# Writing out every engine's order with a small planner in an attention-plus-GLU block

## Chip, cores, metric

One core of one Trainium2 chip. The metric is device time in microseconds (us) of one execution; lower is better. Ratios are the mean time of one kernel's fast runs over that of the other's fast runs of the same rounds, so they are not quite the ratio of the medians quoted beside them. Medians are of all runs, those of state slow included (4 of the changed kernel's 20, and some of the kernel before); ratios and profiles are of fast runs alone, unless the text says otherwise.

## The reference

`x` is 2048 rows of 640 bf16 values. It is normalized once and goes through two branches, which are added to it:

```python
xn = layernorm(x)
q, k, v = split(xn @ wqkv)                # 32 heads of 20
# each position looks at itself and 7 others, 2 rows apart (dilated window of 8)
logits[s, w] = q[s] . k[s - 2*w] * 20**-0.5   # -1e9 where s - 2*w < 0
attn = softmax(logits over w)
A = (sum over w of attn[s, w] * v[s - 2*w]) @ wo
B = ((xn @ w_gate) * (xn @ w_up)) @ w_down    # hidden size 1536
return x + A + B
```

## The kernel before

It works in four chunks of 512 rows (four tiles of 128). Matmuls are on TensorE (PE). The window's products and weighted sums are on VectorE (DVE), PSUM copies on ScalarE (ACT), loads and stores mostly from SyncE's queue (SP). The order on each engine is found by the framework's scheduler from the order of the program. The parts that matter, with cuts:

```python
# the V weights are permuted first thing, ScalarE and GpSimd by turns
for i in range(KT):
    eng = nc.gpsimd.tensor_copy if i % 2 == 0 else nc.scalar.copy
    eng(out=wvp[:, i, :]..., in_=wst[:, i, :]...)

def vproj(c, xnT):
    for ttl in range(CH):
        v_t = cpool.tile([P, D], BF, name="v_t")          # pool default: 2 buffers
        for n0 in (0, N2):
            ...                                           # 5 matmuls into PSUM
            nc.scalar.copy(v_t[:, n0 : n0 + N2], ps[:, 0:N2])
        nc.sync.dma_start(out=vD[...], in_=v_t[:])        # V rows to DRAM

def weights(c):                                           # ... for g in range(2):
    for j in range(JL):                                   # 4 products, 4 buffers
        pt = apool.tile([P, KT, CS], BF, name="pw", tag="pw", bufs=4)
        nc.vector.tensor_tensor(pt[:], qT[:], kT[:, :, off : off + CS], ALU.mult)
    ...                                                   # 20 matmuls sum them by head
    nc.scalar.activation(e[:, g, :], lps[:], ACT.Exp, scale=scale)

def attend(c, ttl):
    v8 = apool.tile([P, W, D], BF, name="v8")             # 8 reloads of V, shifted rows
    for w in range(W):
        nc.sync.dma_start(out=v8[:, w, :], in_=vD[r0 : r0 + P, :])
    ...                                                   # weights, product, three adds

for c in range(NCH):                                      # after chunks 0 and 1 are projected
    for ttl in range(CH):
        attend(c, ttl)
    glu(c)
    if c + 2 < NCH:
        load_x(c + 2); proj(c + 2)
    if c + 1 < NCH:
        weights(c + 1)
    for ttl in range(CH):
        finish(c, ttl)                                    # down and output projection, residual
```

The softmax here doesn't subtract the row's maximum and nothing guards it: scores larger than these inputs give would overflow.

## Time and profile before

| | before |
|---|---|
| median of the first 6 runs | 310.88 us (308.91 to 313.74) |
| span in the profile | 306.5 us |
| first Q matmul to last matmul | 17.5 to 301.2 us |
| dense TensorE work, from pitches (start of one matmul to start of the next) | 265.6 us |

TensorE's dense work (the prediction builds that number) is 87% of the span, so the question is what fills the rest. The lines that show it are in the prediction. In rows of 40 digits each digit is the busy share of one slice of the span in tenths (9 is 90% or more); PEclk is TensorE's granted clock in tenths of full speed. Its columns are line, engine, operation, out<-in, shapes, count; busy time and mean ns; idle time of the engine ahead of it and what ended that:

```profile
L202 ACT CAST v_t<-psv 128x320 bf16<-128x320 f32 x32 | 13.2, 426 | 9.2 <-DMA vD<-v_t 5.5 <-PE psv L197 3.3
```

ScalarE stood 5.5 us, in eight waits, for a store of V to free one of two buffers. In the kernel before nothing behind it was urgent, and no wait of TensorE names it.

### The profile page before, as it was taken

How to read it: one execution, taken by the hardware profiler on the slowest of the kernel's cores; microseconds unless marked ns; L12 is line 12 of the kernel's file. 1: busy time of each engine (PE TensorE's matmuls, PEld its weight loads, DVE VectorE, ACT ScalarE, POOL GpSimd, SP SyncE). 2: the span in 40 equal slices, each digit the busy share in tenths (PEclk: the TensorE clock that was granted, in tenths of full speed). 3: DMA queues.
4: the chain of work that ended last, by engine and by line, in shares of the span. 5: the costliest groups of instructions: out<-in, count | busy, mean ns of one | idle time of the engine just before them, and what ended most of it. 6: DMA issues, size and time to landing. Idle time of an engine off the chain costs nothing.

```text
span 306.5 us, 4647 instructions
## 1 busy us (share of the span) xinstructions
PE 276.0 (90%) x1786; PEld 156.7 (51%) x1786; DVE 196.1 (64%) x277; ACT 123.4 (40%) x221; POOL 45.5 (15%) x92
## 2 busy tenths in 40 slices
PE   0279859999999999999996999999999999999993
PEld 0268524554444467754443467754445674444672
DVE  5223868799988126289999009169999418999311
ACT  1276515655567550035555550025553003555000
POOL 7543000261303001210000001220000121000120
PEclk9999969999999999999999999999999999999999
DMA  7999496825550021225554010225556123540111
GB/s 220 373 370 340 146 288 209 244 90 171 167 150 28 0 88 43 85 84 170 159 172 148 2 64 21 88 86 173 171 171 173 43 87 99 171 118 2 44 51 37
DMA packets 31479, 40.97 MB, mean 134 GB/s; under 512 B 3282, under 2 KB 30432, under 8 KB 31456
## 3 DMA queue, kind: packets, MB, share of 16 engines
q1 hardware_dynamic: 29888, 35.40, 37.3%
q0 software_dynamic: 1568, 5.26, 5.4%
q8 instruction: 14, 0.23, 0.3%
q14 instruction: 9, 0.07, 0.1%
HBM read 35.39 MB, written 5.26 MB: 133 GB/s over the span
## 4 chain that ended last, share of the span: by engine, by line
PE 48%; DVE 31%; DMA 8%; SPq 4%; issue 3%; ACT 3%; POOLq 0%; POOL 0%; DVEq 0%
PE psqk L179 15%; DVE prod L265 13%; DVE pw L223 5%; DVE prod L271 4%; PE psv L197 4%; SPq L243 4%; DMA wst<-in_A_wqkv_dram 3%; DVE hT L303 3%; PE lps L227 3%; DVE prod L272 2%; ACT xnT L160 2%; PE psu L294 2%; PE psg L288 1%; PE pso L277 1%; PE pst L159 1%
## 5 line engine op out<-in xcount | busy, mean ns | idle before, releaser
L223 DVE TENSOR_TENSOR pw<-qT,kT 128x2560 bf16<-128x2560 bf16 x32 | 46.0, 1481 | 25.8 <-ACT v_t L202 14.8
L288 PE MATMUL psg<-xnT,wg 128*128 128x512 bf16 x240 | 60.5, 379 | 0.0
L294 PE MATMUL psu<-xnT,wu 128*128 128x512 bf16 x240 | 60.3, 379 | 0.0
L299 ACT CAST gs<-psg 128x512 bf16<-128x512 f32 x48 | 28.1, 586 | 69.7 <-PE psg L288 36.5
L179 PE MATMUL psqk<-xnT,wqk 128*128 128x512 bf16 (+1 forms) x250 | 45.1, 343 | 0.8 <-ACT xnT L160 0.8
L316 PEld LDWEIGHTS <-hT 128*128 128x128 bf16 x384 | 37.0, 98 | 16.9 <-issue 2.2
L301 ACT CAST us<-psu 128x512 bf16<-128x512 f32 x48 | 28.1, 585 | 23.8 <-PE psu L294 23.5
L294 PEld LDWEIGHTS <-wu 128*128 128x128 bf16 x240 | 23.3, 98 | 26.8
L328 POOL DMA_DIRECT2D out_dram<-osb x16 | 8.8, 550 | 189.5 <-DVE osb L325 178.9
L288 PEld LDWEIGHTS <-wg 128*128 128x128 bf16 x240 | 23.2, 98 | 26.1
L179 PEld LDWEIGHTS <-wqk 128*128 128x128 bf16 x250 | 25.1, 101 | 20.5 <-issue 1.9
L271 DVE TENSOR_TENSOR prod<-prod 128x2560 bf16<-128x2560 bf16 x16 | 23.7, 1484 | 0.0
L197 PE MATMUL psv<-wvp,xnT 128*128 128x320 bf16 x160 | 22.4, 299 | 0.0
L159 PE MATMUL pst<-selb,xn_t 128*128 128x128 bf16 x80 | 8.2, 253 | 15.7 <-POOL rstd L151 9.0
L146 DVE BATCH_NORM_STATS2 stats<-x_t 128x6 f32<-128x320 bf16 x32 | 14.1, 468 | 11.4 <-DMA x_t<-in_A_x_dram 11.3
L303 DVE TENSOR_TENSOR hT<-gs,us 128x512 bf16<-128x512 bf16 x48 | 19.9, 415 | 0.1
L197 PEld LDWEIGHTS <-xnT 128*128 128x128 bf16 x160 | 15.7, 98 | 6.5
L321 PEld LDWEIGHTS <-oT 128*128 128x128 bf16 x160 | 15.6, 98 | 6.6 <-issue 0.6
L227 PE MATMUL lps<-pw,Ek 128*32 128x512 bf16 x160 | 14.9, 409 | 4.3 <-DVE pw L223 4.3
L187 ACT CAST qT<-psqk 128x512 bf16<-128x512 f32 (+1 forms) x25 | 12.5, 500 | 11.9 <-PE psqk L179 11.9
L202 ACT CAST v_t<-psv 128x320 bf16<-128x320 f32 x32 | 13.2, 426 | 9.2 <-DMA vD<-v_t 5.5
L187 ACT CAST kT<-psqk 128x512 bf16<-128x512 f32 (+1 forms) x25 | 12.5, 500 | 9.1 <-PE psqk L179 9.1
(213 smaller groups left out, 291.8 us busy)
## 6 DMA issues: line engine op xcount, KB each, us to landing
x_t<-in_A_x_dram SPq DMA_DIRECT2D x16, 160.0 KB, 4.2
xr<-in_A_x_dram POOLq DMA_DIRECT2D x16, 160.0 KB, 2.6
vD<-v_t SPq DMA_DIRECT2D x16, 160.0 KB, 1.8
out_dram<-osb POOLq DMA_DIRECT2D x16, 160.0 KB, 2.1
wg<-in_B_w_gate_dram SPq DMA_DIRECT2D x2, 960.0 KB, 11.6
wu<-in_B_w_up_dram SPq DMA_DIRECT2D x2, 960.0 KB, 13.4
wd<-in_B_w_down_dram SPq DMA_DIRECT2D x1, 1920.0 KB, 15.6
wqk<-in_A_wqkv_dram SPq DMA_DIRECT2D x2, 800.0 KB, 7.1
```

The costliest lines, as they stand in the source:

```text
L179: nc.tensor.matmul(ps[:, 0:n], lhsT=wqk[:, i, r * D + j * P : r * D + (j + 1) * P], rhs=xnT[:, i, t0 : t0 + n], start=(i == 0), stop=(i == ...
L187: nc.scalar.copy(dst[:, j, o : o + n], ps[:, 0:n])
L197: nc.tensor.matmul(ps[:, 0:N2], lhsT=xnT[:, i, tcols(ttl)], rhs=wvp[:, i, n0 : n0 + N2], start=(i == 0), stop=(i == KT - 1),)
L223: nc.vector.tensor_tensor(pt[:], qT[:], kT[:, :, off : off + CS], ALU.mult)
L265: nc.vector.tensor_tensor(prod[:].rearrange("p w (j h) -> p w j h", j=Dh, h=H), v8[:].rearrange("p w (j h) -> p w j h", j=Dh, h=H), a16[:, ...
L271: nc.vector.tensor_tensor(prod[:, 0:4, :], prod[:, 0:4, :], prod[:, 4:8, :], ALU.add)
L288: nc.tensor.matmul(pg[:], lhsT=wg[:, i, f * P : (f + 1) * P], rhs=xnT[:, i, :], start=(i == 0), stop=(i == KT - 1),)
L294: nc.tensor.matmul(pu[:], lhsT=wu[:, i, f * P : (f + 1) * P], rhs=xnT[:, i, :], start=(i == 0), stop=(i == KT - 1),)
L299: nc.scalar.copy(gs[:], pg[:])
L301: nc.scalar.copy(us[:], pu[:])
L303: nc.vector.tensor_tensor(h[:], gs[:], us[:], ALU.mult)
L316: nc.tensor.matmul(ps[:, 0:N2], lhsT=hT[f][:, tcols(ttl)], rhs=wd[:, f, n0 : n0 + N2], start=(f == 0), stop=False,)
```

## The change

The intent: TensorE should never stand for the attention chain of VectorE. The automatic order is switched off for all five engines. A small planner in the kernel simulates TensorE and VectorE with assumed durations while the program is built, and emits each operation at the moment when its simulated engine is free. TensorE has a main list of blocks (Q/K, V, gate/up, final projection); head sums, spreads and transposes ("burst") go between blocks when the plan says their input is ready. VectorE has one chain; gate products and residuals ("quick") slip in. PSUM is shared out anew, gate copies have 2 buffers (were 3), `e` has 2 (was 1), `oT` 6 (were 5). GpSimd forms 1/std for two or four tiles at once. The core of the diff, with cuts:

```diff
-    ps_log = ctx.enter_context(tc.tile_pool(name="ps_log", bufs=2, ...))
+    ps_log = ctx.enter_context(tc.tile_pool(name="ps_log", bufs=1, ...))
+    ps_e = ctx.enter_context(tc.tile_pool(name="ps_e", bufs=1, ...))
+    ctx.enter_context(tc.manual_schedule(engines={PE, DVE, Activation, SP, Pool}))
...
+    zt = cpool.tile([P, D], BF, name="zt", tag="v_t")   # zeros ahead of V; had a buffer of its own
...
+    def load_w1():
+        load_x(1)
+        ...                       # wg, wu in halves, then wo_perm, then wd
...
+    def run():
+        t = {"pe": 8.0, "dve": 3.0}
+        while main or chain or burst or quick:
+            ...
+            eng = "pe" if t["pe"] <= t["dve"] else "dve"
+            extra, base = (burst, main) if eng == "pe" else (quick, chain)
+            extra.sort(key=lambda o: o[3]())
+            pick = None
+            if extra and extra[0][3]() <= t[eng]:
+                pick = extra.pop(0)
+            elif base and base[0][3]() <= t[eng]:
+                pick = base.popleft()
+            ...
+            name, emit, took, _, after = pick
+            emit()
+            t[eng] += took
+            done[name] = t[eng] + 0.2
...
+                def product(g=g, j=j):
+                    pt = apool.tile([P, KT, CS], BF, name="pw", tag="pw", bufs=4)
...
+                def after(t, g=g, j=j, heads=heads, headed=headed):
+                    if j == JL - 1:
+                        burst.append((("heads", c, g), heads, 1.2, lambda t=t: t + 0.4, headed))
+                dve(("pw", c, g, j), product, 1.45, when(("qk", c)), after)
...
+    norm(0, 2)
+    side(load_w1)
+    norm(1, 4)
+    side(lambda: [permute_v(i, nc.gpsimd.tensor_copy if i % 2 == 0 else nc.scalar.copy)
+                  for i in range(KT)])
     weights(0)
+    side(lambda: (want_v8(0), want_v8(1), load_x(2)))
+    norm(2, 4)
+    attend(0)
+    weights(1)
+    side(lambda: load_x(3))
+    norm(3, 4)
+    attend(1)
+    weights(2)
+    weights(3)
+    attend(2)
+    attend(3)
+
+    qk(0, 2); vproj(0); qk(1, 1); vproj(1); glu(0); finish(0)     # one call a line
+    qk(2, 1); vproj(2); qk(3, 1); vproj(3); glu(1); finish(1)     # in the kernel
+    glu(2); finish(2); glu(3); finish(3)
+    run()
```

## The prediction

> **What bounds the kernel now.** I read the page's head and slices first, then the chain that ended last for the pitch of each kind of matmul, then stretches where a slice showed TensorE short of full, and last the timeline of VectorE in an attention stretch.
>
> ```profile
> PE 276.0 (90%) x1786; PEld 156.7 (51%) x1786; DVE 196.1 (64%) x277; ACT 123.4 (40%) x221; POOL 45.5 (15%) x92
> PE   0279859999999999999996999999999999999993
> DVE  5223868799988126289999009169999418999311
> PEclk9999969999999999999999999999999999999999
> ```
>
> A slice is 306.5/40 = 7.7 us. PE is full except in the first two slices, the stretch of slices 4 to 5 and one digit 6 at about 161 us. DVE swings between 9 and 0: it has 110 us of idle time in all, but stretches in which it is the full engine. So TensorE bounds the kernel, with holes where it waits for VectorE, ScalarE and the start.
>
> The 276.0 is an overlapping count, so I build the dense time from pitches in the chain (start, length, what, how many matmuls):
>
> ```profile
> 3.69 10.11 DMA wst<-in_A_wqkv_dram
> 13.82 2.54 ACT wvp L133 x2
> 17.70 12.03 PE psqk L179 x100
> 47.05 10.99 PE psqk L179 x50
> 83.15 1.08 PE psg L288 x5
> 106.48 5.43 PE psv L197 x40
> 111.91 1.19 PE lps L227 x20
> 117.83 1.63 PE pso_1357 L316 x12
> 119.46 0.68 PE pso_1357 L321 x5
> ```
>
> Sum: Q and K 12.03 + 3 x 10.99 = 45.0; V 4 x 5.43 = 21.7; gate and up 4 x 24 x 1.08 = 103.7; output projection 32 x (1.63 + 0.68) = 73.9; head sums 8 x 1.19 = 9.5; 32 groups of five transposes at about 0.3 (start-to-start 56 to 66 ns) = 9.6; 32 small matmuls that spread the weights at 0.07 = 2.2. Together 265.6 us. Dense work runs from 17.0 to 301.4 us = 284.4, so holes after the start cost about 19 us; 17.0 go by before it and 5.1 (residual, store, landing) after it.
>
> Two of those lines say where the start goes: ScalarE permuted the V weights (waiting 10 us for their load) ahead of the copies that the first Q matmul needed. The larger holes (stretch, then busy of PE, PEld, DVE, ACT, POOL, clock, DMA):
>
> ```profile
> 35.00:47.00 12.00, 7.72 (x64) 3.57 (x63) 7.61 (x10) 4.41 (x8) 0.00 (x0) 0.72 0.85 252
> 160.00:167.00 7.00, 4.42 (x51) 2.49 (x51) 6.92 (x10) 4.38 (x7) 0.00 (x0) 1.00 0.64 188
> 38.53 0.38 PE L227 MATMUL lps<-pw,Ek 128*32 128x512 bf16 x1 [0.83 <-DVE pw L223]
> 42.73 2.29 PE L227 MATMUL lps<-pw,Ek 128*32 128x512 bf16 x17 [0.82 <-DVE pw L223]
> ```
>
> In the first, PE takes its head sums one product at a time as DVE makes them (1.4 us each), and the granted clock fell to 0.72. Its useful work there is 2.4 head sums + 1.3 transposes + 0.2 spread, about 4 us of 12: 8 lost. In the second about 4 are lost: transposes wait for the last attention output. Some 3 to 4 more go near 231 to 240 us (head sums again), 2 near 93, and about 0.4 for most attention outputs.
>
> **What the Trainium skill says.** "TensorE: Matmul & The Clock Gate", Part 1, gives start-to-start of N/2.4 GHz + 2.5 ns warm, half the clock cold, warm after about 3.4 us of activity. The trace agrees: 216 ns at N=512, 136 at 320, 109 at 256, and 213 at N=256 in the first 2.3 us of Q. A dense block can't be improved by order; a cold start costs a little over 1 us wherever it falls. The same page (architectural detail) has the queues of ScalarE, VectorE and GpSimd as strict FIFO; the trace agrees in that 10 us ScalarE wait with ready copies behind it. So the written order is binding: one operation too early stops everything behind it. "Perfetto Trace Analysis", Optimization Strategy, advises interleaving regimes with different busiest engines; that is the change's aim.
>
> **The change part by part.** Arithmetic, shapes and instruction counts stay, but for GpSimd's rstd on two or four tiles at once.
>
> *Start.* x lands from 3.07 us (first statistics). Two tiles' statistics end at 5.3, rstd about 6.4, scaling 7.4, transposes and two 0.69 copies about 8.9. The first half of the Q/K weights was issued at 2.64 and landed 6.2 later: 8.8. Permuting V no longer stands ahead. Q can start at about 9.0 in place of 17.5: 8.5 gained. Against it: V weights land at 13.8 but are permuted only behind the statistics of chunk 1, whose x lands after them, about 14; 4.3 of statistics, 1.0 of rstd, then GpSimd's three copies of 1.30 end near 23, while PE could start V at about 21. Loss 2 to 3.
>
> *Attention threaded.* The order on PE is Q/K and V of chunks 0 and 1, gate/up 0, projection 0, Q/K/V 2 and 3, then gate/up and projection 1, 2, 3; head sums, transposes and spreads are put between blocks about when VectorE should have delivered. VectorE gets one chain, with gate products and residuals slipped in.
>
> ```profile
> 261.98 0.36 DVE L254 RECIPROCAL rs<-eT 128x32 f32<-128x32 f32 x1 [0.35 <-PE eT L249]
> 262.37 0.42 DVE L256 TENSOR_TENSOR a_2868<-eT,rs 128x256 bf16<-128x256 f32 x1
> 262.83 2.83 DVE L265 TENSOR_TENSOR prod<-v_2854,a_2868 128x5120 bf16<-128x5120 bf16 x1
> 265.91 1.48 DVE L271 TENSOR_TENSOR prod<-prod 128x2560 bf16<-128x2560 bf16 x1
> 267.65 0.82 DVE L272 TENSOR_TENSOR prod<-prod 128x1280 bf16<-128x1280 bf16 x1
> 268.50 0.49 DVE L274 TENSOR_TENSOR o_2874<-prod 128x640 bf16<-128x640 bf16 x1
> ```
>
> By start-to-start, one tile without gate products takes 0.39 + 0.46 + 2.75 + 1.40 + 0.74 + 0.41 = 6.15 us; the planner assumes 0.75 + 2.8 + 1.45 + 0.8 + 0.45 = 6.25. Products are 1.40 against 1.45, gate products 0.33 against 0.4; its PE blocks 1.08, 0.68 and 17 x 0.136 = 2.31 equal the chain's. So the plan should hold. Laying its chain along the PE order by hand: products of chunk 0 from about 24 us, attention 0 about 42 to 73 while projection 0 is due at 77; attention 1 ends near 125, needed at 160; attention 2 near 180, just ahead of projection 2; attention 3 has 30 us of slack. VectorE never has to be the bound.
>
> *New or remaining waits on PE.* (a) V permutation: 2.5. (b) Four product buffers: the fifth product of a chunk waits for the first head sum (0.4 lag + half a block 0.5 + 1.2 + 0.2 = 2.3 us), which the planner doesn't count; the second head sum stands in PE's order 0.9 after the planned product, so PE waits 1.4 less what VectorE gained on the plan (2 to 3%), about 0.8 x 4 = 3. (c) Four normalization transposes share two PSUM buffers with 0.69 us copies: 0.7 x 3 = 2. (d) Projection's last gate products, held behind a 2.8 us operation: 0.7 x 3 = 2. (e) Placing the other 40 or so insertions, at 0.05: 2. Sum 11.5, in place of 19.
>
> *Sum.* 9.0 + 265.6 (its Q of chunk 0 holds the cold start; less 0.7 for two transpose groups before it) + 11.5 + 5.1 = 290.5 us of span, 16 below. The six timed runs' median lies 4.4 above the profiled span and the profiled run itself 1.75; with 2.5 to 3: 293.
>
> **The rivals.** (1) *VectorE becomes the bound.* Its 196.1 us busy are far below 290, and the plan's constants are slightly long. But PE is in order, so every lag is a PE stall; if the chain lags 2 us at each of its 24 stages (chunks' products, tiles), some 15 us return: 305. The 0 digits of DVE in the old slices speak against it: there is slack to fill. (2) *PE runs nearly dense*: the waits (b) to (e) fall within the slack, and 4 us remain: 283 of span, 286. For it, the constants look calibrated on this chip; against it, the buffers are as few as before, and fewer for head sums (PSUM 2 to 1) and gate copies (3 to 2). (3) *The start is bandwidth-bound*: DMA share is 1.06 and 364 GB/s between 17 and 30 us. If x of chunk 1 or the V copies come late, (a) grows to 6: 297.
>
> **Range and chances.** The eight gained at the start are the safest part; the holes at 35 to 47 and 160 to 167 are nearly as safe, since other PE work is ordered there. Giving back all of it needs rival 1 in full. I take 293, with 286 (rival 2) and 302 (most of rival 1) as ends. Faster by over 2% (below 304.7): 0.94; within 2%: 0.05; slower: 0.01.
>
> **What would show it.** Right: first Q matmul near 9 us; V of chunk 0 starts 2 us or so after Q and K end; no PE digit under 9 from slice 4 on; the clock stays at full after its warm-up; DVE's zeros fill until about 215 us and then thin out; PE's leftover waits name pw, the xnT copies and gate products, a few us together; last matmul near 285. Wrong: waits of 1 us or more at most attention transposes, a second clock drop, or gate-copy waits on ScalarE that pass to PE through full PSUM buffers.

## The result, and the profile after

The changed kernel took 310.46 us (20 runs, 308.17 to 314.17), the kernel before 309.75 us in 40 runs; ratio 1.0021, 95% interval 0.9997 to 1.0045. No change, where 293 was predicted. The page of the changed kernel, the lines that answer to the prediction's first fence:

```profile
span 309.4 us, 4637 instructions
PE 277.3 (90%) x1786; PEld 157.9 (51%) x1786; DVE 202.3 (65%) x277; ACT 122.1 (39%) x221; POOL 32.0 (10%) x70
PE   0888498999999979968998999999999999999993
DVE  2783457799997669998078899989982381221211
PEclk9999989999999979995999999999999999999998
```

The holes of before (35 to 47 us and 161 us) are gone, but others stand in slices 4, 14 and 17 (counted from 0: digits 4, 7 and 6), the first of them near 33 us; the clock has three visible drops instead of one; and from slice 22 on (170 us) PE is at 9 to the end. VectorE's two zeros (slices 22 and 23) are filled, though a new one stands in slice 19 (147 to 155 us), and it has little to do in the last quarter, as planned.

The intended order is there, then; what is not there is its time. I set the plan's start of a block (printed while the kernel is built) beside the chip's start of the same block (the trace; TensorE runs its matmuls in order, so the count of matmuls finds the block). This is the most useful table; "five edits" is a later experiment, 8, against its own plan:

| first matmul of | plan | chip | chip late | with five edits, late by |
|---|---|---|---|---|
| Q/K of chunk 0 | 9.50 | 10.23 | 0.7 | 0.7 |
| V of chunk 0 | 22.22 | 27.16 | 4.9 | 4.3 |
| Q/K of chunk 1 | 27.66 | 37.14 | 9.5 | 4.3 |
| gate/up of chunk 0 | 47.89 | 61.58 | 13.7 | 5.5 |
| Q/K of chunk 2 | 98.89 | 116.95 | 18.1 | 5.6 |
| Q/K of chunk 3 | 116.12 | 134.01 | 17.9 | 7.4 |
| V of chunk 3 | 127.51 | 152.43 | 24.9 | 7.3 |
| gate/up of chunk 2 | 185.73 | 214.01 | 28.3 | 7.0 |
| final projection of chunk 3 | 257.66 | 285.68 | 28.0 | 6.6 |

The lag grows in jumps, and is flat between them: the assumed durations are right, and the whole loss is in a few events. The largest are at 33 and 136 us. First the chain that ended last (start, length, what), at both places:

```profile
29.36 7.21 DMA vD<-v_t
37.14 4.01 PE psqk L290 x10
136.16 3.87 DMA vD<-v_t
140.61 8.47 PE psqk L290 x25
```

A store of V stands in the chain just ahead of Q/K matmuls, which need nothing of V. The timeline of ScalarE (start, length, engine, line, operation, count, and in brackets the idle time before it and what ended it) shows the link, and that of SyncE shows why the second store was late:

```profile
30.26 0.43 ACT L326 CAST v_t<-psv 128x320 bf16<-128x320 f32 x1 [0.20 <-PE psv L321]
36.67 1.41 ACT L326 CAST v_t<-psv 128x320 bf16<-128x320 f32 x4 [5.98 <-DMA vD<-v_t]
140.13 0.75 ACT L326 CAST v_t<-psv 128x320 bf16<-128x320 f32 x2 [6.85 <-DMA vD<-v_t]
140.77 0.60 ACT L298 CAST qT<-psqk 128x512 bf16<-128x512 f32 x1
```

```profile
130.59 0.32 SPq L328 DMA_DIRECT2D vD<-v_t  x1
132.42 3.64 SPq L343 DMA_DIRECT2D v_1560<-vD  x8
136.16 5.07 SPq L328 DMA_DIRECT2D vD<-v_t  x3
```

Near 33 us: the store was issued at 29.36 and landed 7.2 us later, while the weight loads were still coming in. The third V tile needed its buffer, so ScalarE stood for 5.98 us; behind it stood the copies that free PSUM; so TensorE stood 4.2 us with its data ready. Near 136 us the store itself was late: the second V tile of its chunk was complete at 131.9 us, but ahead of its store in SyncE's queue stood the eight reloads for the chunk's first tile, which waited until 132.4 for the landing of the store issued at 130.59 (they read those rows) and then took 3.64 us to issue. (The expectation of experiment 1 puts their wait down to a VectorE product. That is what other reloads wait for; this one waited for the landing.) ScalarE stood 6.85 us and TensorE 4.0.

At the end of each wait the granted clock fell to half (at 37.3 and 139.7 us). In this view of stretches the columns are length, busy time and count of PE, PEld, DVE, ACT, POOL, then clock, DMA share and GB/s:

```profile
136.00:147.00 11.00, 7.00 (x20) 2.51 (x19) 9.88 (x8) 3.55 (x8) 0.00 (x0) 0.69 0.72 218
```

Summed over the trace (start-to-start times above the warm pitches, waits put to what ended them; my arithmetic from the trace's rows):

| TensorE time, us | before | after | five edits |
|---|---|---|---|
| dense | 263.4 | 263.4 | 263.4 |
| wait for ScalarE at a V buffer | 0 | 8.5 | 0 |
| head sums wait for products | 5.8 | 5.5 | 0 |
| other waits over 0.25 | 16.4 | 8.7 | 7.4 |
| small gaps | 3.6 | 1.6 | 1.0 |
| lost to half clock | 3.0 | 8.2 | 2.9 |
| start of first matmul | 9.0 | 8.1 | 8.1 |
| start of last matmul | 301.2 | 304.0 | 282.8 |

So the change did remove 7.7 us of other waits (6.5 of those of before stood at the start), 2 of small gaps and 0.9 of start, and gave 8.5 to a new wait and 5.2 to the clock.

### The profile page after: what moved, and what is told of

Its sections match the earlier page's. It is cut to its first block, busy times and chain, and to the rows that moved or that the text cites. A ratio compares the mean times of both kernels' runs of the same rounds, so it can differ in the third digit from the quotient of the medians.

```text
span 309.4 us, 4637 instructions
## 1 busy us (share of the span) xinstructions
PE 277.3 (90%) x1786; PEld 157.9 (51%) x1786; DVE 202.3 (65%) x277; ACT 122.1 (39%) x221; POOL 32.0 (10%) x70
## 4 chain that ended last, share of the span: by engine, by line
PE 63%; DVE 14%; DMA 8%; issue 7%; ACT 3%; SPq 2%; POOL 1%; POOLq 0%; DVEq 0%; ACTq 0%
PE psu L504 14%; PE psg L504 14%; PE psf L549 12%; PE psqk L290 10%; PE psf L542 5%; DVE pw L360 5%; DMA vD<-v_t 4%; PE psv L321 4%; DMA x_t<-in_A_x_dram 3%; PE lps L371 2%; DVE stats L223 2%; DVE prod L444 2%; DVE xn_t L241 1%; PE pso L470 1%; SPq L343 1%
## 5 line engine op out<-in xcount | busy, mean ns | idle before, releaser
L290 PE MATMUL psqk<-xnT,wqk 128*128 128x512 bf16 (+1 forms) x250 | 51.6, 367 | 9.0 <-ACT v_t L326 8.2
L504 PE MATMUL psg<-xnT,wg 128*128 128x512 bf16 x240 | 59.6, 379 | 0.0
L549 PE MATMUL psf<-wd,hT 128*128 128x320 bf16 x384 | 58.2, 301 | 0.4 <-DVE hT L514 0.4
L549 PEld LDWEIGHTS <-hT 128*128 128x128 bf16 x384 | 37.9, 99 | 15.8 <-DVE hT L514 0.7
L290 PEld LDWEIGHTS <-wqk 128*128 128x128 bf16 x250 | 25.9, 105 | 31.5 <-issue 16.5
L460 DVE TENSOR_TENSOR prod<-prod 128x2560 bf16<-128x2560 bf16 (+1 forms) x32 | 36.9, 1153 | 0.4
L557 DVE TENSOR_TENSOR osb<-psf,xr 128x320 bf16<-128x320 f32 x32 | 15.6, 487 | 26.0 <-PE psf L549 22.1
L542 PE MATMUL psf<-wo_perm,oT 128*128 128x320 bf16 x160 | 27.7, 305 | 0.0
L321 PE MATMUL psv<-wvp,xnT 128*128 128x320 bf16 x160 | 23.4, 299 | 1.1 <-ACT kT L298 1.0
L472 ACT COPY oT<-pso 128x640 bf16<-128x640 bf16 x16 | 11.2, 697 | 26.8 <-PE pso L470 26.7
L298 ACT CAST qT<-psqk 128x512 bf16<-128x512 f32 (+1 forms) x25 | 12.6, 503 | 17.5 <-PE psqk L290 17.5
## 6 DMA issues: line engine op xcount, KB each, us to landing
wg<-in_B_w_gate_dram SPq DMA_DIRECT2D x2, 960.0 KB, 10.2
```

Of the source, the lines that this page charges most:

```text
L290: nc.tensor.matmul(ps[:, 0:n], lhsT=wqk[:, i, r * D + j * P : r * D + (j + 1) * P], rhs=st["xnT"][:, i, t0 : t0 + n], start=(i == 0), stop ...
L298: nc.scalar.copy(dst[:, j, o : o + n], ps[:, 0:n])
L321: nc.tensor.matmul(ps[:, 0:N2], lhsT=st["xnT"][:, i, tcols(ttl)], rhs=wvp[:, i, n0 : n0 + N2], start=(i == 0), stop=(i == KT - 1),)
L460: nc.vector.tensor_tensor(prod[:, 0:k, :], prod[:, 0:k, :], prod[:, k : 2 * k, :], ALU.add)
L504: nc.tensor.matmul(ps[:], lhsT=w[:, i, f * P : (f + 1) * P], rhs=st["xnT"][:, i, :], start=(i == 0), stop=(i == KT - 1),)
L542: nc.tensor.matmul(ps[:, 0:N2], lhsT=st["oT", ttl][:, i, :], rhs=wo_perm[:, i, n0 : n0 + N2], start=(i == 0), stop=False,)
```

## The experiments

My theory, called the queue theory in the expectations: TensorE is the bound, and the loss is a handful of waits in in-order queues that the plan doesn't know of, with the clock drops as their consequence. Rivals: VectorE's chain is the bound, so that a released TensorE waits for it; or the clock drops have a cause of their own. Ten kernels ran, all gave correct results, and each except one (on the kernel before) is an edit of the changed kernel. They ran in three groups, each on one chip: experiments 1, 2, 4, 5 (beside them the kernel before took 310.27 us), 6, 7, 8, 10 (309.52), and 3, 9 (311.02). Six of the traces lack 19 or 20 of 1786 matmul records, so positions from those are good to a block. The gains of experiments 1, 3 and 4 are clear of noise, but their intervals straddle 0.98: that they exceed 2% is not settled.

### 1. V stores from ScalarE's queue

```diff
-                        nc.sync.dma_start(
+                        nc.scalar.dma_start(
                             out=vD[HALO + tg * P : ...], in_=v_t[:])
```

> One edit to the changed kernel: the 16 stores of V rows are issued from ScalarE's own queue, right behind the copy that fills their buffer, and no longer stand in SyncE's queue behind the reloads of V that wait for a VectorE product. Queue theory (the changed kernel is bound by TensorE, and loses 8.5 us because ScalarE stands still for a V buffer whose store is late, 4.4 near 33 us and 4.2 near 136 us, and about 5 more because the clock halves after each): both PE waits and both drops go, PE ends 9 to 13 us earlier, time 297 to 301. Rival, the VectorE chain is the bound: PE is released earlier but waits for products instead, time 308 or more. Rival, the clock drops have another cause: waits go, drops at 37 and 140 us stay, time about 302.

Measured 303.86 us, ratio 0.979 (0.974 to 0.983): 6.4 us, little more than half of what I expected. The wait near 136 us is gone, and the clock drop behind it too. The first wait stayed:

```profile
37.69 0.75 ACT L326 CAST v_t<-psv 128x320 bf16<-128x320 f32 x2 [5.03 <-DMA vD<-v_t]
```

The first store left ScalarE's queue at 31.33, with nothing ahead of it there, and still landed 6.3 us later. The Trainium skill says so ("DMA: Bandwidth & Descriptors", Issuing engines are not separate DMA queues): whichever engine issues them, DMAs run on the same 16 DMA engines and interleave. Another queue cures waiting to be issued, not waiting for the DMA engines.

### 2. Four V buffers

```diff
-    v_t = cpool.tile([P, D], BF, name="v_t")
+    v_t = cpool.tile([P, D], BF, name="v_t", bufs=4)      # the same for zt, which shares the tag
-    h = cpool.tile([P, CS], BF, name="hT", bufs=14)
+    h = cpool.tile([P, CS], BF, name="hT", bufs=12)      # makes the room
```

> Another way to the same end: V buffers 2 to 4 (gate product buffers 14 to 12 to make room), stores left in SyncE's queue. A chunk has four V tiles, so ScalarE never waits for a store inside a chunk. Queue theory: same gain as with the stores moved, time 297 to 301. If only the place in the queue mattered and not the count, it gains under 3 us. VectorE rival: 308 or more.

Measured 298.47 us, ratio 0.961 (0.957 to 0.965). ScalarE never waits for a store, and TensorE's two waits at the V buffer are gone:

```profile
136.00:147.00 11.00, 10.95 (x84) 6.33 (x84) 9.40 (x7) 6.98 (x14) 0.00 (x0) 1.00 0.50 150
```

The same stretch has a full PE (10.95 in place of 7.00 us) at full clock. This is 12 us from a change of two numbers, in line with 8.5 of wait and about 4 of half clock. It also speaks against both rivals: VectorE had the slack to follow, and the drops at 37 and 140 us went with the waits. The other drops are not settled by it: the one at 112 us is gone too, although the wait before it is still there (1.13 us), and one appeared at 24.5 us, after waits for the slowed scalings of experiment 5 that the changed kernel has too, at full clock. Experiment 6 returns to this.

### 3. Weights for the down projection loaded behind the first V stores

```diff
-        nc.sync.dma_start(out=wd[:], ...)                 # last in load_w1
...
-    side(lambda: (want_v8(0), want_v8(1), load_x(2)))
+    side(lambda: (want_v8(0), want_v8(1), load_x(2), load_wd()))
```

> One edit to the changed kernel: the load of the down-projection weights (1.9 MB) is issued behind the first V stores instead of ahead of them; two V buffers and SyncE's queue as in the changed kernel. If the first stores land late because the DMA engines still have weights to bring, as the like landing times in four runs suggest (36.6 to 38.5 us, from either queue), they now land 2 to 3 us after issue, the PE wait of 4.4 near 33 us and the clock drop behind it go, the wait near 136 us stays: 303 to 306. If the late landing has another cause, 309 to 311.

Measured 305.32 us (three fast runs, one slow), ratio 0.979 (0.969 to 0.990). The first store landed about 2 us after its issue at 31.28:

```profile
33.17 0.80 ACT L328 CAST v_t<-psv 128x320 bf16<-128x320 f32 x2 [0.56 <-DMA vD<-v_t]
```

So the first store was late because of 1.9 MB of weights ahead of it in the DMA engines. The wait near 136 us (4.2 us of PE) stayed, as expected: the two V waits have different causes, and only the buffer count, experiment 2, removes both.

### 4. The planner told of the product buffers

```diff
                 def headed(t, g=g):
                     done[("exp", c, g)] = t + 0.9
+                    done[("free pw", c, g)] = t
...
-                dve(("pw", c, g, j), product, 1.45, when(("qk", c)), after)
+                need = [("qk", c)]
+                if j == 0 and (g == 1 or ("first", c) in held):   # c >= 1
+                    need.append(("free pw", c, 0) if g else held[("first", c)])
+                dve(("pw", c, g, j), product, 1.45, when(*need), after)
```

`held[("first", c)]` is the second head sum of the chunk before.

> The planner is told of the four product buffers: the first product of each group of four may start only when the head sum before it is done, so TensorE gets other blocks in that time instead of standing at the second head sum. Queue theory: the waits of head sums for products (5.5 us on PE in the changed kernel) go, gain 3 to 5, time 305 to 307, lag of the chip behind the plan no longer grows at head sums. VectorE rival: same waits move elsewhere, time 309 to 311.

Measured 305.43 us, ratio 0.984 (0.977 to 0.991), though the V waits were still there. In the changed kernel PE stopped inside the second head sum; here it runs Q/K matmuls until the products are there, and the head sum goes through in one piece. Two lines of the changed kernel:

```profile
46.70 0.40 PE L371 MATMUL lps<-pw,Ek 128*32 128x512 bf16 x3
48.12 1.24 PE L371 MATMUL lps<-pw,Ek 128*32 128x512 bf16 x17 [1.03 <-DVE pw L360]
```

and one of this:

```profile
48.62 1.26 PE L372 MATMUL lps<-pw,Ek 128*32 128x512 bf16 x20
```

No instruction and no buffer was changed, only the planner's knowledge. VectorE waits for its buffers as before; TensorE no longer does.

### 5. The permutation of the V weights moved

```diff
     side(load_w1)
+    side(lambda: [permute_v(i, nc.gpsimd.tensor_copy) for i in (0, 2, 4)])
     norm(1, 4)
-    side(lambda: [permute_v(i, ...) for i in range(KT)])
+    later.append((lambda: permute_v(1, nc.scalar.copy), lambda: 15.0))
+    later.append((lambda: permute_v(3, nc.scalar.copy), lambda: 17.5))
```

> The permutation of the V weights moved: GpSimd's three copies ahead of chunk 1's normalization, ScalarE's two one at a time about 15 and 17.5 us of the plan. Chunk 1's scaling is then not slowed by GpSimd's copies (0.45 us each instead of up to 1.44) and V starts near 23 in place of 27 us. But the first V store lands when the weight loads ahead of it have drained, at about 36.5 us, whenever it is issued. Queue theory: V starts 3 to 4 us earlier and the wait for the store grows by as much; time 309 to 311, no gain. If the losses simply add up, 306.

Measured 311.22 us, ratio 1.002 (0.996 to 1.009): no gain, as expected, but the parts differ. V started at 26.5, only 0.7 us earlier (I had expected 3 to 4), and the store landed 10 us after its issue, at 38.5 and not at 36.5, so that the wait for it grew to 8.73 us of ScalarE and 6.96 of PE. Why it landed later is open:

```profile
38.55 1.41 ACT L326 CAST v_t<-psv 128x320 bf16<-128x320 f32 x4 [8.73 <-DMA vD<-v_t]
```

The cause that the move removes is real. VectorE's scaling of chunk 1's x while GpSimd copies, in the changed kernel, and with the copies elsewhere, here:

```profile
19.00 4.50 DVE L241 TENSOR_SCALAR xn_t<-x_t,mv,rstd 128x640 bf16<-128x640 bf16 x4 [1.47 <-POOL rstd L227]
```

```profile
20.45 0.81 DVE L241 TENSOR_SCALAR xn_t<-x_t,mv,rstd 128x640 bf16<-128x640 bf16 x2 [1.48 <-POOL rstd L227]
```

A scaling takes 0.45 us alone, but up to 1.44 beside GpSimd's copies of 1.38 each. "SBUF — State Buffer", Who interferes with whom, has the mechanism: VectorE (in a two-port mode, which a bf16 `tensor_scalar` can take) and GpSimd share a port pair that one holds for a whole instruction while the other blocks. The trace agrees: the slow ones last one GpSimd copy each.

### 6. Residual loads from ScalarE's queue

```diff
-                            nc.gpsimd.dma_start(
+                            nc.scalar.dma_start(
                                 out=st["xr"][:], ...)
```

> One edit to the changed kernel: the loads of the residual rows are issued from ScalarE's queue instead of GpSimd's, where one stood behind the rstd of chunk 3 until 106.9 us, so that VectorE stood 3.7 us at a residual and TensorE then waited for the scaled x (3.3 us in all at these transposes) and its clock halved at 112 us. Queue theory: residual waits under 0.5, PE waits for scaled x near 109 us gone, gain 3 to 5, time 305 to 307. If these waits are hidden by the later ones (the V store near 136 us), no gain: 309 to 311.

The wait it aims at, in the changed kernel's timeline: the load stood in GpSimd's queue behind chunk 3's 1/std, and VectorE stood behind the load, with the scaling that TensorE needed next in line.

```profile
106.92 0.62 POOL L535 DMA_DIRECT2D xr<-in_A_x_dram  x1
109.59 0.49 DVE L557 TENSOR_TENSOR osb<-psf,xr 128x320 bf16<-128x320 f32 x1 [3.74 <-DMA xr<-in_A_x_dram]
```

Measured 308.82 us, ratio 0.997 (0.990 to 1.005; it fits the three runs without the profiled one); two runs fast (304.73, profiled, and 307.94), two slow. In the profiled run VectorE no longer stands at the residual, and TensorE's waits for scaled x near 109 us (1.08 and 0.30) are gone, so the wait is explained; that it is worth time by itself is not shown. (The 3.3 us of the expectation also hold waits at 22 us, 1.6 of them.)

That the clock drop at 112 us is gone here proves nothing: experiments 1, 2 and 5 keep the wait (1.14, 1.13 and 1.06 us) and have no drop there either. In all twelve traces the changes of the clock lie on a grid of 3.41 us, whose place differs from run to run. In the changed kernel TensorE's wait near 33 us left one stretch of that grid almost empty (33.89 to 37.30: PE busy for 0.16 us), and the clock halved. Here the same wait (3.69 us) fell across two stretches (30.92 to 34.34 and 34.34 to 37.75: busy for 1.58 and 1.55), and the clock stayed full. This edit touches neither that wait nor the grid, so part of the 304.73 is luck.

### 7. Experiments 2 and 4 together

> The two edits that gained alone, together: four V buffers and the planner told of the product buffers. Alone they gave about 12 and 5 us. Queue theory: they act on separate waits and add up, 293 to 295. If they share a wait (VectorE's chain running late), 297 to 298.

Measured 291.10 us, ratio 0.939 (0.933 to 0.944): better than the sum of the two alone (12 and 5 us, 293 to 295). Once TensorE never stands for long, the clock stays full after its start: 0.997 in the mean of the profiled run (0.991 to 0.999 in the four), against 0.974 in the changed kernel's (0.968 to 0.988 in its 21).

### 8. All of 1, 2, 4, 5, 6

> All five edits: stores of V and loads of the residual from ScalarE's queue, four V buffers, product buffers in the plan, permutation of V moved. Now V can start earlier and nothing stands behind the first store, so the permutation's 3 us should show, and the residual's 3. Queue theory: 286 to 290, PE waits under 8 us in sum, one drop of the clock at most. If VectorE's chain binds once the waits are gone: 293 or more with waits of PE for products, scaled x and attention outputs.

Measured 288.93 us, ratio 0.932 (0.926 to 0.937).

```profile
span 287.5 us, 4631 instructions
PE 269.2 (94%) x1786; PEld 155.6 (54%) x1786; DVE 199.1 (69%) x277; ACT 121.9 (42%) x221; POOL 23.2 (8%) x54
PE   0798999999999999899999999999999999999993
PEclk9999999999999999999999999999999999999999
```

PE is at 9 but for the start, one digit and the end, at full clock. The plan-against-chip table above has its lag: 6.6 us at the end in place of 28.0.

### 9. Only 2, 4 and 5

> Best kernel less the two moves to ScalarE's queue: four V buffers, product buffers in the plan, V permutation moved; V stores stay with SyncE and residual loads with GpSimd. If the count of V buffers has made the store's queue irrelevant, it equals the kernel with all five edits or is at most 2 slower: 288 to 291, and the permutation is worth 1 to 3 on top of the pair that took 291.1. If the queue still matters, 293 or more.

Measured 288.98 us, ratio 0.931 (0.926 to 0.937): the same. With four V buffers, moving stores and residual loads to another queue adds nothing that shows. The permutation, worth nothing alone, may be worth about 2 us on top of experiment 7 (291.10; other chip, but both beside the kernel before: 0.931 against 0.939, with intervals that overlap; experiment 8, on the chip of 7, took 288.93). The traces don't show it: the last matmul starts at 282.9 us in experiment 7 and at 282.8 in experiment 8. These three edits are the version to keep; it beats the kernel before by 6.9%, and so the changed kernel, which equals that one, by about as much.

### 10. The kernel before, V weights permuted by GpSimd alone

```diff
-        eng = nc.gpsimd.tensor_copy if i % 2 == 0 else nc.scalar.copy
+        eng = nc.gpsimd.tensor_copy
```

> The kernel before with one edit and no planner: all five copies that permute the V weights on GpSimd, so ScalarE doesn't stand for their load ahead of the first normalized x. PE's first Q matmul near 11 to 12 in place of 17.5 us. If the start is worth its whole length, 304 to 305; if the stretch from 35 to 47 us (VectorE making products one by one, chunk 1's x late) is set by loads and VectorE, the gain is given back there: 308 to 310. The second is expected, for the kernel before had both.

Measured 306.26 us, ratio 0.988 (0.982 to 0.995). The first Q matmul came at 11.68 in place of 17.5 us, 5.8 earlier, and 3.3 of that reached the end. I had expected 308 to 310, less gain than it brought. The hole after V moved with the start (29 to 45 us, PE waiting for products one by one) and the clock was at half for 13.7 us there. So the earlier start alone does not close that hole; the kernels with the planner's order don't have it.

## Why the prediction was wrong, point by point

**What bounds the kernel** was right: TensorE, with dense work of 265.6 us (263.4 warm plus its cold start). Experiments 2, 7 and 8 confirm it, for the time followed TensorE's waits one for one or better.

**The start** was nearly right: first Q matmul at 10.2, predicted 9.0. The transposes ran on a cold clock and their two copies ended 1.2 us later than I had it. The cold clock cost more than "a little over 1 us": 2.0 us in the changed kernel and 2.9 in experiment 8. One line was misread, without weight in the sum: 10.11 us is the length of the load of the V weights; ScalarE itself stood 3.4 us for it, not 10, and TensorE 5.8 us for the copies that did stand behind.

**VectorE is never the bound** was right. Attention of all chunks was ready when its projection was due, shifted with TensorE.

**The sum of waits on TensorE is the step that failed.** I listed five and summed 11.5 us. Measured from first Q to the end: (a) V permutation 2.5 predicted, 2.8 found (1.6 for slowed scalings, 1.2 for PSUM behind ScalarE's copies; by another mechanism than the queue of GpSimd alone). (b) Product buffers 3 predicted, 5.5 found: I counted on VectorE gaining on the plan between chunks; the second head sums of chunks 0 and 1 cost about their full 1.4 each (1.3), and three later ones 0.5, 1.6 and 0.8. (c) Transposes and ScalarE's copies 2 predicted, 1.1 found, and 1.7 more near 109 us from the residual load, which I had not seen. (d) Last gate products 2 predicted, 0.5 found. (e) Small insertions 2 predicted, some 3 found. Not listed at all: ScalarE's wait for V buffers, 8.5 us of TensorE, and the clock that halved three times after the start, about 6. These two are 14.5 of the 18.6 us by which the last matmul came late (304.0 against 285.4).

I could have seen the first. The row shown names the wait; I left it out as it cost TensorE nothing, but the new order puts the Q/K of the next chunk straight behind V, so that ScalarE's next copies became urgent. I had also written that an operation too early stops everything behind it in a queue, and applied it to the orders of ScalarE and GpSimd at the start only, not to SyncE's queue, where the new order puts V stores behind weight loads and reloads of V. The prediction's last line named the right path (ScalarE, then full PSUM buffers), but for gate copies.

**The rivals**: rival 1 came nearest in size (305, measured 310.5), for the wrong reason; its sum doesn't come out either, since 2 us at 24 stages are 48 and not 15. Rival 2, nearly dense with 286, is what experiments 8 and 9 came near (289). Rival 3, the start bound by loads, had its term (a) wrong (2.8, not 6), but loads did cost time at the start, by way of the V store that took 7.2 us to land.

**What stays open**: the last 6.6 us of lag. About 4 of it arises before V of chunk 0, some 3 of that with the cold clock. Why runs of one kernel keep more or less of the clock (experiment 6: 0.994 in one run, 0.975 in three) was not tried; where the grid of 3.41 us falls on the waits is a likely reason, not a tested one.

## What to carry to other kernels

A hand-written order is only as good as the list of things that it knows: buffers, and every in-order queue including the DMA issuer, belong in the planner as much as durations. Put the plan's times beside the trace's: flat stretches say that durations are right, and each jump points at one wait that the plan doesn't know. When one engine serves several users, a wait that cost nothing before becomes the bound as soon as the new order places something urgent behind it.

## What the Trainium skill lacked or had wrong

- "TensorE: Matmul & The Clock Gate", HAM oscillation, puts the rule as no idle gaps over about 3.4 us. Shorter gaps sufficed here: in the changed kernel the clock halved at 112.4 us, after 3.4 us in which PE was busy for 1.75 with transposes and no wait was over 1.3; with four V buffers it halved at 24.5 us after waits of at most 0.9 (busy 1.41 of 3.4). It stayed full in experiment 8 through a stretch busy for 2.22 of 3.4. The page lacks how busy is busy enough. I laid the grid of clock changes (experiment 6) over all twelve traces (961 stretches), between first and last matmul and at full clock, with transposes counted as busy: all 13 stretches of 3.41 us in which PE was busy for 1.46 us or less were followed by half clock, none with 1.81 or more was, and two of the five between were. Of the 21 us by which experiment 7 brought the last matmul forward, 6 were half clock.
- "DMA: Bandwidth & Descriptors", Anatomy of one DMA, gives about 2 us of fixed cost, fitted for DMAs issued from GpSimd. It lacks a figure for a small store behind bulk loads: a 160 KB store landed in 1.8 us at best but in 6.3 to 10.0 us while weight loads were coming in, from either issuing queue.
- "SBUF — State Buffer", Who interferes with whom, has the shared port pair right and gives bare factors ("DVE 6.8× slower"); it lacks how long an operation of known size gets: a 0.45 us VectorE scaling of 128x640 took up to 1.44 (3.2 times) beside GpSimd copies of 1.38.
